# Results of two head groups packed into 32 rows, and VectorE's score blocks in threes, in a two-branch attention kernel

## The chip, the cores and the metric

The kernel runs on one core of a Trainium2 chip, as one program on its five engines: TensorE (PE in the profile), VectorE (DVE), ScalarE (ACT), GpSimd (POOL) and SyncE (SP), which issues the DMA transfers. The metric is the device time of one execution in microseconds (us). The kernel before took 934.92 us, the median of three runs (931.52, 934.92 and 940.07).

## What is computed

```python
def reference(A_x, A_wqkv, A_wo, B_x, B_wqkv, B_wo, gate_w):
    # B = 1, S = 2048, D = 512, H = 32 heads of Dh = 16
    def _A_ref(x, wqkv, wo):          # full attention
        q, k, v = split_heads(x @ wqkv)
        p = softmax(einsum("bhqd,bhkd->bhqk", q, k) * Dh ** -0.5)
        return merge_heads(einsum("bhqk,bhkd->bhqd", p, v)) @ wo
    def _B_ref(x, wqkv, wo):          # each query sees 8 keys, 2 apart, ending at itself
        q, k, v = split_heads(x @ wqkv)
        idx = pos[:, None] - 2 * arange(8)[None, :]
        logits = where(idx >= 0, einsum("bhsd,bhswd->bhsw", q, k[idx]) * Dh ** -0.5, -1e9)
        return merge_heads(einsum("bhsw,bhswd->bhsd", softmax(logits), v[idx])) @ wo
    g = sigmoid((A_x * gate_w).sum(-1, keepdims=True))
    return g * _A_ref(A_x, A_wqkv, A_wo) + (1 - g) * _B_ref(A_x, B_wqkv, B_wo)
```

All inputs and the output are bf16. Both branches read A_x. The work is the full attention of branch A: 32 heads x 2048 x 2048 scores and as many exponentials.

## The kernel before

**Tiling.** The 2048 queries are four chunks of 512. The 32 heads are eight groups of four (i = 0 to 7); the four heads j of a group lie in the four 32-row strips of the 128 partitions, 16 rows of data in each strip. A *period* is one head group on one chunk. There are 32: chunks 0 and 1 alternate through the eight groups (periods 0 to 15), then chunks 2 and 3 (16 to 31). A *block* is the scores of one head, 128 keys by 512 queries; a period has 64 of them (16 key tiles x 4 heads).

**The way of a block on ScalarE.** Blocks go in sets of 3 and 2 in turn. `qk` (L909) puts the scores of a set into one of two PSUM rings (tiles ring, rA of three banks and rB of two), one matmul a block; `ex` (L915) takes the exponential of the whole set in one ScalarE instruction into a tile pT (three buffers for each ring); `pv` (L928, through `pv_mm`, L876) multiplies each block with V and a column of ones into the accumulator acc, of which there is one PSUM bank. This leaves the result and the softmax's denominator of the four heads in acc, 17 rows of each strip.

**The way of a block on VectorE.** Some blocks of each period (`n_dve`, L20, 116 in all) are not given to ScalarE. `d_group` (L946, called from L1008) handles them in groups of up to two: `dq` puts the scores of one block into one of the two PSUM banks called misc, `p1` turns them to a scaled number in dt (one VectorE instruction a block), and `p2`, `p3` and `p4` form the exponential from it for the whole group (dg<-dt, dg<-dt,dg and pd<-dg,dt, scalar_tensor_tensor instructions over 512 elements a partition for each block of the group); `pv` multiplies pd into acc (called dpv). Each `dq` waits for the `p1` of the block before it. dt, dg and pd have one buffer each.

**The end of a period.** VectorE turns acc in 32 x 32 blocks into accT (`po1`), takes the reciprocal of the denominators (`pr`), multiplies (`po2`, L1028) into half of each 32-wide row of ott2, whose other half is zero, and turns ott2 back (`po3`, L1033) into its head group's plane of the tile oat. A plane has 128 rows, of which only 16 of each 32 carry data; woarr holds the matching rows of A_wo, with zeros in the others, so that the output product (`a_mm`, L1052, and `a_steps`, L1069; PE's misc_ps<-woarr,oat) takes eight planes, four matmuls of 32 output rows for each, for every 128 queries.

**Output.** For chunks 0 to 2 each tile of 128 queries is done once its chunk's last period is over: product with woarr (pf), scaled by the gate into fa, product of branch B with bwo (pb), sum into osb, store. For chunk 3, branch B's part is put into fb early, planes 0 to 3 (pf) and 4 to 6 (pg) are added to it by `fa_ev` (L1115) as they come, and after the last period only plane 7 (pt) is left.

**Branch B** runs beside all that, in 16 tiles (`b_tile`, L649) planned 46.7 us apart: projections on PE, products and weighted sums on POOL (prod, ob, obb), small steps on VectorE.

**Projections.** `q_proj` (L534, called from L586) makes the queries of one period into a tile qt (three buffers), `k_proj` the keys kt_all of one head group and chunk; both use the misc banks and VectorE.

**The order.** Every piece is an `Op` with an engine, an expected duration, a due time, dependencies and tokens for the buffers it takes (a token of a resource can only be given when the users of an older one are done). `list_schedule` (L80) lays all of them out in time with these expected durations, adds products with zeros where PE would otherwise be idle (acc<-ones_t,z, `zeros`), and the program is issued in that order; on each engine it is strict, and semaphores wait where a buffer or a result is not there yet. A changed duration, buffer count or due time so changes the order on every engine.

Of the kernel before, what the change touches and what calls it, by code (L numbers as in the profile page):

```python
# [9 lines left out]
ALU = mybir.AluOpType  # L10
# [8 lines left out]
    chunks_at_once=2,  # L19
    n_dve=(3,) * 14 + (2,) * 4 + (4,) * 9 + (6,) * 5,  # L20
    dve_tiles=2,
# [6 lines left out]
DH = 16  # L28
NG = 8
# [153 lines left out]
def kernel(  # L183
# [21 lines left out]
    NBG = S // 32  # L205
    BPC = QW // 32
    SZ = cfg["set_sizes"]
    NTD = cfg["dve_tiles"]
# [99 lines left out]
    z_scr = tc.dram_tile([S], FP32, name="z_scr")  # L308
    woarr = const.tile([128, NG, D], BF16, name="woarr")
    ident = const.tile([128, 128], BF16, name="ident")  # L310
# [24 lines left out]
    def init_dve():  # L335
        V.memset(selq[:], 0.0)
        V.memset(rowc[:], 0.0)
        for j in range(4):
            V.memset(selq[32 * j:32 * j + DH, 32 * j + DH:32 * j + DH + 1], 1.0)
            V.memset(rowc[32 * j:32 * j + DH + 1, 1:2], 1.0)  # L340
            V.memset(rowc[32 * j:32 * j + DH + 1, 2:3], SHIFT)
            V.memset(rowc[32 * j:32 * j + DH, 0:1], 1.0)
            V.memset(rowc[32 * j:32 * j + DH, 1:3], 0.0)
        V.memset(ott2[:], 0.0)

# [3 lines left out]
    def init_pool2():  # L349
        make_identity(nc, identf[:])  # L350
        G.memset(vp_all[:, 0, :, :], 1.0)
        G.memset(vp_all[:, 1:NT, :, DH:DH + 1], 1.0)

    def init_pool3():
        G.memset(woarr[:], 0.0)

# [3 lines left out]
    o_init_p = op("pool", 2.8, init_pool2, -8.0, deps=[o_id])  # L360
    o_wz = op("pool", 3.6, init_pool3, -7.0, deps=[o_init_p])

# [3 lines left out]
    def load_x(sc):  # L366
        def s():
            if sc < 2:
                xl = work.tile([128, W, D], BF16, name="xld", tag="prod", bufs=2)
            else:  # L370
                xl = work.tile([128, NG, QW], BF16, name="xld2", tag="oat", bufs=2)
            SP.dma_start(out=xl[:, 0:TPC, :], in_=x2d[sc * QW:(sc + 1) * QW, :].rearrange("(t p) d -> p t d", p=128))
            xld[sc] = xl
        return s
# [11 lines left out]
    def load_wo():  # L386
        SP.dma_start(out=bwo[:], in_=B_wo.rearrange("(c p) n -> p c n", p=128))
        wo4 = A_wo.rearrange("(i j d) n -> j d i n", j=4, d=DH)
        for j in range(4):
            SP.dma_start(out=woarr[32 * j:32 * j + DH, :, :], in_=wo4[j])  # L390
        SP.dma_start(out=v_scr[0:16, :], in_=woarr[16:32, 0, :])

# [9 lines left out]
    o_bw = op("sp", 1.0, load_bw, -8.3, lat=14.5)  # L402
    o_wo = op("sp", 3.5, load_wo, -8.2, deps=[o_wz], lat=17.0)

# [129 lines left out]
    def q_proj(pi, tag, dl, rel=0.0):  # L534
        c_, i = periods[pi]
        st = {}
        tk = tok(tag, 2 if tag == "misc" else 1)
        tq = tok("qt", 3)
        ta = tok("absq", 1)
        q_tok[pi] = tq  # L540

        def part(c0, c1):
            def s():
                if c0 == 0:
                    st["p1"] = misc_ps([128, QW], tag=tag)
                    st["absq"] = work.tile([128, QW], BF16, name="absq", tag="absq", bufs=1)
                    qt_tiles[pi] = work.tile([128, QW], BF16, name="qt", tag="qt", bufs=3)
                for c in range(c0, c1):
                    mm_heads(st["p1"], c, 4 * i * DH, xT[:, c, c_ * QW:(c_ + 1) * QW], c == 0, c == DC - 1)
            return s  # L550
# [34 lines left out]
    for pi in range(1, NP):  # L585
        q_proj(pi, "misc", S0[pi] - 16.0, rel=S0[pi - 1] + 4.0 if pi == 1 else S0[pi - 1] - 4.0)  # L586

# [311 lines left out]
    for k, us in enumerate(sets):  # L899
# [4 lines left out]
        tr_ = tok(ring, 1)  # L904
        tp = tok("pT" + ring, 3)
        tn = T0 + UNIT * sum(SZ) * (k // 2) + (UNIT * SZ[0] if k % 2 else 0)
# [8 lines left out]
        def ex(us=us, st=st, ring=ring, maxn=maxn, n=n):  # L915
            st["p"] = work.tile([128, maxn, QW], BF16, name="pT", tag="pT" + ring, bufs=3)
            A.activation(out=st["p"][:, 0:n, :], in_=st["r"][:, 0:n, :], func=ACT.Exp, scale=float(DH) ** -0.5)
# [25 lines left out]

    d_last = [None]

    def d_group(pi, gr, lo, hi):  # L946
        c_, i = periods[pi]
        n = len(gr)
        st = {}
        td, tg, tp = tok("dt", 1), tok("dg", 1), tok("pd", 1)  # L950

# [9 lines left out]
        def p1(q_):  # L961
            def s():
                if q_ == 0:
                    st["dt"] = work.tile([128, 2, QW], FP32, name="dt", tag="dt", bufs=1)
                    st["fr"] = st["dt"][:].bitcast(U16).rearrange("p u (n two) -> p u n two", two=2)[:, 0:n, :, 0]
# [4 lines left out]
        def p2():  # L970
            st["dg"] = work.tile([128, 2, QW], BF16, name="dg", tag="dg", bufs=1)
            V.scalar_tensor_tensor(out=st["dg"][:, 0:n, :], in0=st["fr"], scalar=EXP_A, in1=st["fr"],
                                   op0=ALU.subtract, op1=ALU.mult)
# [5 lines left out]
        def p4():  # L979
            st["pd"] = work.tile([128, 2, QW], BF16, name="pd", tag="pd", bufs=1)  # L980
            V.scalar_tensor_tensor(out=st["pd"][:, 0:n, :].bitcast(U16), in0=st["dg"][:, 0:n, :], scalar=EXP_C,
# [6 lines left out]
        def dur(t):  # L988
            return 0.15 + 0.535 * n + ((0.2 + 0.16 * n) if in_b(t) else 0.05)
        prev = d_last[0]  # L990
        for q_, (t, j) in enumerate(gr):
            tx = tok("misc", 2)
            a = op("pe", 0.28, dq(q_), hi - 7.5 + q_, dense=0.75, deps=[o_q[pi], o_kc[i][t // TPC], prev] + ([o_k0[t // TPC]] if i == 0 else []), alloc=[tx], use=[q_tok[pi]],
                   rel=lo, lat=0.52, name=f"dq{pi}")
            prev = op("dve", 0.70, p1(q_), hi - 6.5 + q_, deps=[a], alloc=[td] if q_ == 0 else [],
                      use=[tx] + ([td] if q_ else []))
        d_last[0] = prev
        a = op("dve", dur, p2, hi - 4.2, deps=[prev], alloc=[tg], use=[td])
# [5 lines left out]
    for pi in range(NP):  # L1004
        gs = [dorder[u_:min(u_ + 2, n_dve[pi])] for u_ in range(0, n_dve[pi], 2)]
        plen = S0[pi + 1] - S0[pi]
        for m, gr in enumerate(gs):
            d_group(pi, gr, S0[pi] - 6.0, S0[pi] + 1.0 + (plen - 7.0) * (m + 1) / len(gs))  # L1008


    oat_tiles, oat_tok, o_oat = {}, {}, {}
    for pi, (c_, i) in enumerate(periods):
        st = {}
        if i == 0:
            oat_tok[c_] = tok("oat", 2)
        ta, to = tok("accT", 2), tok("ott", 2)
        E = S0[pi + 1]
# [9 lines left out]

        def po2(pi=pi, st=st):  # L1028
            rden = st["rden"]
            rd_bc = _ap(rden[:], [list(rden[:].ap[0]), [1, BPC], [0, DH]])  # L1030
            V.tensor_tensor(out=ott2[:, pi % 2, :, 0:DH], in0=st["a"][:, :, 0:DH], in1=rd_bc, op=ALU.mult)

        def po3(pi=pi, c_=c_, i=i):  # L1033
            if c_ not in oat_tiles:
                oat_tiles[c_] = work.tile([128, NG, QW], BF16, name="oat", tag="oat", bufs=2)
            V.transpose(out=oat_tiles[c_][:, i, :], in_=ott2[:, pi % 2].rearrange("p b d -> p (b d)"))
        prev = [o_oat[pi - 1]] if pi else []
        a = op("dve", 0.75, po1, E - 1.0, deps=o_pv[pi], alloc=[ta], use=[acc_tok[pi]])
        a = op("dve", 0.27, pr, E + 3.5, deps=[a], use=[ta])
        a = op("dve", 0.60, po2, E + 4.0, deps=[a], alloc=[to], use=[ta])  # L1040
        o_oat[pi] = op("dve", 0.74, po3, E + 6.0, deps=[a] + prev, alloc=[oat_tok[c_]] if i == 0 else [],
                       use=[to] + ([oat_tok[c_]] if i else []))

    st_fb = {}
    for t in range(NT):
# [41 lines left out]
        if not last:  # L1087
# [7 lines left out]
            def b_ev(st=st, t=t):  # L1095
# [3 lines left out]
                                       op0=ALU.mult, op1=ALU.add)  # L1099
            a, tk = a_steps("pf", 0, NG, dl - 2.0, [o_oat[PL], o_g, o_wo] + o_obt[TPC * c_:TPC * (c_ + 1)], [oat_tok[c_]])  # L1100
            tf = tok("accT", 2)
# [34 lines left out]
        o_fb = op("dve", 0.70, fb_ev, dl + 1.0, deps=[a, o_g], alloc=[] if tt else [tfb], use=[tk] + ([tfb] if tt else []))  # L1136
        dl = S0[NP - 3] + 5.0 * tt
        a, tk = a_steps("pf", 0, 4, dl, [o_oat[p_of[c_, 3]], o_fb, o_g], [oat_tok[c_]])
        a = op("dve", 0.75, fa_ev("pf"), dl + 1.0, deps=[a, o_fb], use=[tk, tfb])
        dl = S0[NP - 1] + 8.0 + 3.0 * tt  # L1140
        b, tk = a_steps("pg", 4, NG - 1, dl, [o_oat[p_of[c_, NG - 2]], a], [oat_tok[c_]])
        a = op("dve", 0.75, fa_ev("pg"), dl + 1.0, deps=[a, b], use=[tk])
        tag = ("misc", "acc", "misc", "rA")[tt]
        tk, tos = tok(tag, 2 if tag == "misc" else 1), tok(otag, obufs)
        E2 = S0[NP]
        b = op("pe", 0.26, a_mm("pt", NG - 1, NG, True, True, tag=tag), E2 + tt, deps=[o_oat[NP - 1], a], alloc=[tk], use=[oat_tok[c_]])
        b = op("dve", 0.70, t_ev, E2 + 1 + tt, deps=[b, a], alloc=[tos], use=[tk, tfb])
# [39 lines left out]
```

## Time and profile before

| | before |
|---|---|
| median of three runs | 934.92 us |
| profiled execution | 930.82 us |
| its span, first to last instruction | 929.0 us |
| ScalarE busy | 890.4 us (96%) |
| TensorE busy | 837.3 us (90%) |
| VectorE busy | 656.9 us (71%) |
| GpSimd busy | 524.9 us (57%) |
| mean granted TensorE clock | 0.99 |
| exponentials of score sets on ScalarE | 773, 880.5 us in all |

Lines of groups read: engine, operation, what is written <- what is read by the program's names, shapes (partitions x elements), number of instructions, then busy us and mean ns of one, then the engine's idle time just before them and what ended it. Nearly every instruction goes through one recording helper, so the line number (L240, L249) says little and the tile's name says which step it is. In lines of stretches each engine has its busy us and its instructions in brackets; after the engines stand the granted clock of TensorE as a share, the share of the DMA engines, and GB/s. In lines of waits the three figures are us in total, times and the longest.

### The profile page before, as it was taken

How to read it: one execution, taken by the hardware profiler on the slowest of the kernel's cores; microseconds unless marked ns; L12 is line 12 of the kernel's file. 1: busy time of each engine (PE TensorE's matmuls, PEld its weight loads, DVE VectorE, ACT ScalarE, POOL GpSimd, SP SyncE). 2: the span in 40 equal slices, each digit the busy share in tenths (PEclk: the TensorE clock that was granted, in tenths of full speed). 3: DMA queues.
4: the chain of work that ended last, by engine and by line, in shares of the span. 5: the costliest groups of instructions: out<-in, count | busy, mean ns of one | idle time of the engine just before them, and what ended most of it. 6: DMA issues, size and time to landing. Idle time of an engine off the chain costs nothing.

```text
span 929.0 us, 20631 instructions
## 1 busy us (share of the span) xinstructions
PE 837.3 (90%) x8716; PEld 312.5 (34%) x8716; DVE 656.9 (71%) x880; ACT 890.4 (96%) x799; POOL 524.9 (57%) x412
## 2 busy tenths in 40 slices
PE   7999999989998999989999988888989898889887
PEld 4333334333433334333333432332323322222222
DVE  4676787887588777776436575778687876577676
ACT  4999999999999999999998999999999999999994
POOL 3445682868558748685854393989694993000000
PEclk9999999999999999999999999999999989999999
DMA  9101010010101010100012001010110010000001
GB/s 272 53 2 52 2 53 2 7 46 7 52 3 47 22 37 2 52 24 30 6 65 69 13 2 52 1 52 2 52 47 7 1 46 1 1 1 2 1 1 47
DMA packets 27269, 28.62 MB, mean 31 GB/s; under 512 B 1540, under 2 KB 26660, under 8 KB 27176
## 3 DMA queue, kind: packets, MB, share of 16 engines
q1 hardware_dynamic: 27176, 27.30, 9.2%
q8 instruction: 68, 1.11, 0.5%
q14 instruction: 25, 0.20, 0.1%
HBM read 23.08 MB, written 4.22 MB: 29 GB/s over the span
## 4 chain that ended last, share of the span: by engine, by line
ACT 50%; issue 20%; PE 20%; DVE 9%; DMA 1%; SPq 0%; ACTq 0%; DVEq 0%
ACT pT L240 49%; PE misc_ps L249 6%; PE ring L249 6%; PE acc L249 5%; DVE dg L240 4%; DVE pd L240 1%; PE misc L249 1%; DVE dt L240 1%; DMA xld<-in_A_x_dram 1%; ACT lg L240 1%; DVE osb L240 0%; DVE qt L240 0%; DVE accT L240 0%; DVE vd_all L240 0%; DVE ott L240 0%
## 5 line engine op out<-in xcount | busy, mean ns | idle before, releaser
L240 ACT ACTIVATE pT<-ring 128x1536 bf16<-128x1536 f32 (+1 forms) x773 | 880.5, 1347 | 15.5 <-PE acc L249 8.4
L249 PE MATMUL ring<-qt,kt_all 32*128 32x512 bf16 x1932 | 307.9, 383 | 72.4 <-ACT pT L240 65.7
L249 PE MATMUL acc<-pT,vp_all 128*17 128x512 bf16 (+1 forms) x1932 | 306.1, 385 | 0.6 <-DVE accT L240 0.2
L249 PEld LDWEIGHTS <-kt_all 32*128 32x128 bf16 x2048 | 114.3, 91 | 343.8 <-issue 330.4
L240 POOL TENSOR_TENSOR prod<-kTb,qTb 128x512 f32<-128x512 bf16 x128 | 165.0, 1311 | 106.4 <-DVE qTb L240 84.6
L240 POOL TENSOR_TENSOR prod<-vsh,lg 128x512 f32<-128x512 bf16 x128 | 170.5, 1355 | 0.8
L240 DVE TENSOR_SCALAR dt<-misc 128x512 f32<-128x512 f32 x116 | 79.7, 687 | 71.5 <-PE misc L249 65.6
L240 POOL TENSOR_TENSOR prod<-prod 128x512 f32<-128x512 f32 x80 | 122.7, 1549 | 1.3
L249 PEld LDWEIGHTS <-vp_all 128*17 128x17 bf16 (+1 forms) x1932 | 67.8, 88 | 122.6 <-issue 113.2
L240 DVE SCALAR_TENSOR_TENSOR pd<-dg,dt 128x1024 uint16<-128x1024 bf16 x65 | 98.3, 1513 | 1.7 <-PE acc L249 0.6
L240 DVE SCALAR_TENSOR_TENSOR dg<-dt,dg 128x1024 bf16<-128x1024 uint16 x65 | 96.3, 1482 | 1.6
L249 PE MATMUL misc_ps<-xT,wst 128*32 128x512 bf16 x1024 | 94.0, 382 | 1.1 <-ACT kt_all L240 0.8
L240 DVE SCALAR_TENSOR_TENSOR dg<-dt 128x1024 bf16<-128x1024 uint16 x65 | 91.8, 1412 | 1.7
L240 POOL TENSOR_TENSOR lg<-lg,rr 128x256 f32<-128x256 f32 x16 | 10.4, 648 | 126.8 <-ACT pT L240 60.0
L249 PE MATMUL acc<-ones_t,z 128*32 128x512 bf16 x211 | 74.6, 393 | 0.0
L249 PE MATMUL misc<-qt,kt_all 32*128 32x512 bf16 x116 | 44.9, 387 | 0.9 <-DVE kt_all L240 0.6
L249 PE MATMUL misc_ps<-woarr,oat 128*32 128x512 bf16 x512 | 44.1, 382 | 1.6 <-DVE fa L240 1.6
L249 PE MATMUL misc_ps<-prod,hsel 128*32 128x128 f32 x1024 | 42.9, 279 | 0.7 <-DVE kt_all L240 0.3
L249 PE MATMUL misc_ps<-xT,bw 128*128 128x128 bf16 x512 | 38.5, 220 | 0.0
L249 PEld LDWEIGHTS <-bw 128*128 128x128 bf16 x512 | 28.8, 98 | 14.7 <-issue 14.1
L249 PEld LDWEIGHTS <-wst 128*32 128x32 bf16 x1024 | 25.5, 95 | 22.2 <-issue 10.7
L249 PE MATMUL acc<-pd,vd_all 128*17 128x512 bf16 x116 | 27.6, 382 | 5.1 <-DVE pd L240 3.2
(86 smaller groups left out, 608.3 us busy)
## 6 DMA issues: line engine op xcount, KB each, us to landing
vsh<-v_scr SPq DMA_DIRECT2D x16, 1024.0 KB, 5.1
xld<-in_A_x_dram SPq DMA_DIRECT2D x4, 512.0 KB, 4.0
v_scr<-vs SPq DMA_DIRECT2D x16, 128.0 KB, 1.7
out_dram<-osb SPq DMA_DIRECT2D x16, 128.0 KB, 1.7
wst<-in_A_wqkv_dram SPq DMA_DIRECT2D x3, 512.0 KB, 8.8
bw<-in_B_wqkv_dram SPq DMA_DIRECT2D x1, 1536.0 KB, 11.2
bwo<-in_B_wo_dram SPq DMA_DIRECT2D x1, 512.0 KB
woarr<-in_A_wo_dram SPq DMA_DIRECT2D x4, 128.0 KB, 11.8
```

The lines of the kernel that those rows point to most:

```text
L240: return chain_on(key, f(*a, **k))
L249: return chain(nc.tensor.matmul(out, lhsT=lhsT, rhs=rhs, start=start, stop=stop, **kw))
```

## The change

The 16 rows of an odd head group go into the free half of the rows of the even one before it. `po2` of group i writes half i % 2 of the rows of ott2 (which is still one tile for each of the two chunks at work), and `po3` turns it back once for two groups, after the odd one. So oat and woarr have four planes and no zero rows, the output product is four planes long, and chunk 3's has two parts in place of three: planes 0 to 2 ahead of time, plane 3 at the end. woarr is loaded in eight transfers of 64 KB in place of four of 128 KB, is not zeroed any more, and the zero rows for the head of v_scr come from a tile osb that POOL zeroes.

VectorE's blocks go in groups of up to three of near equal size (a period with 3 blocks has one group, with 5 a pair and a triple, with 6 two triples), and there are 129: 3 each in periods 0 to 17, 5 each in 18 to 26, 6 each in 27 to 31. `dq` waits for the `p1` of the block before the last one. pd gets three buffers, pT four for each ring, qt four. A group may start 25 us ahead of its period's planned start in place of 6, and the queries are due 4 us earlier and may start 8 us earlier. The expected duration of `p2` to `p4` while branch B runs changes from 0.35 + 0.695 us x blocks to 0.51 + 0.535 us x blocks.

```diff
-    n_dve=(3,) * 14 + (2,) * 4 + (4,) * 9 + (6,) * 5,
+    n_dve=(3,) * 18 + (5,) * 9 + (6,) * 5,
...
+    NP2 = NG // 2
...
-    woarr = const.tile([128, NG, D], BF16, name="woarr")
+    woarr = const.tile([128, NP2, D], BF16, name="woarr")
...
-        V.memset(ott2[:], 0.0)
...
-        G.memset(woarr[:], 0.0)
+        st_z["z"] = work.tile([128, D], BF16, name="osb", tag="osb", bufs=2)
+        G.memset(st_z["z"][0:16, :], 0.0)
...
-        wo4 = A_wo.rearrange("(i j d) n -> j d i n", j=4, d=DH)
-        for j in range(4):
-            SP.dma_start(out=woarr[32 * j:32 * j + DH, :, :], in_=wo4[j])
-        SP.dma_start(out=v_scr[0:16, :], in_=woarr[16:32, 0, :])
+        wo5 = A_wo.rearrange("(m s j d) n -> s j d m n", s=2, j=4, d=DH)
+        for s_ in range(2):
+            for j in range(4):
+                SP.dma_start(out=woarr[32 * j + DH * s_:32 * j + DH * (s_ + 1), :, :], in_=wo5[s_][j])
+        SP.dma_start(out=v_scr[0:16, :], in_=st_z["z"][0:16, :])
...
-        tq = tok("qt", 3)
+        tq = tok("qt", 4)
...
-        q_proj(pi, "misc", S0[pi] - 16.0, rel=S0[pi - 1] + 4.0 if pi == 1 else S0[pi - 1] - 4.0)
+        q_proj(pi, "misc", S0[pi] - 20.0, rel=S0[pi - 1] + 4.0 if pi == 1 else S0[pi - 1] - 12.0)
...
-        tp = tok("pT" + ring, 3)
+        tp = tok("pT" + ring, 4)
...
-        td, tg, tp = tok("dt", 1), tok("dg", 1), tok("pd", 1)
+        td, tg, tp = tok("dt", 1), tok("dg", 1), tok("pd", 3)
...
-            return 0.15 + 0.535 * n + ((0.2 + 0.16 * n) if in_b(t) else 0.05)
-        prev = d_last[0]
+            return 0.15 + 0.535 * n + (0.36 if in_b(t) else 0.05)
+        prev2, prev = d_last
         for q_, (t, j) in enumerate(gr):
             tx = tok("misc", 2)
-            a = op("pe", 0.28, dq(q_), hi - 7.5 + q_, dense=0.75, deps=[o_q[pi], o_kc[i][t // TPC], prev] + ([o_k0[t // TPC]] if i == 0 else []), alloc=[tx], use=[q_tok[pi]],
+            a = op("pe", 0.28, dq(q_), hi - 7.5 + q_, dense=0.75, deps=[o_q[pi], o_kc[i][t // TPC], prev2] + ([o_k0[t // TPC]] if i == 0 else []), alloc=[tx], use=[q_tok[pi]],
...
-        gs = [dorder[u_:min(u_ + 2, n_dve[pi])] for u_ in range(0, n_dve[pi], 2)]
+        ng = -(-n_dve[pi] // 3)
+        gs = [dorder[m * n_dve[pi] // ng:(m + 1) * n_dve[pi] // ng] for m in range(ng)]
...
-            d_group(pi, gr, S0[pi] - 6.0, S0[pi] + 1.0 + (plen - 7.0) * (m + 1) / len(gs))
+            d_group(pi, gr, S0[pi] - 25.0, S0[pi] + 1.0 + (plen - 7.0) * (m + 1) / len(gs))
...
-            V.tensor_tensor(out=ott2[:, pi % 2, :, 0:DH], in0=st["a"][:, :, 0:DH], in1=rd_bc, op=ALU.mult)
+            V.tensor_tensor(out=ott2[:, pi % 2, :, DH * (i % 2):DH * (i % 2 + 1)], in0=st["a"][:, :, 0:DH], in1=rd_bc, op=ALU.mult)
...
-            V.transpose(out=oat_tiles[c_][:, i, :], in_=ott2[:, pi % 2].rearrange("p b d -> p (b d)"))
+            V.transpose(out=oat_tiles[c_][:, i // 2, :], in_=ott2[:, pi % 2].rearrange("p b d -> p (b d)"))
...
-        o_oat[pi] = op("dve", 0.74, po3, E + 6.0, deps=[a] + prev, alloc=[oat_tok[c_]] if i == 0 else [],
-                       use=[to] + ([oat_tok[c_]] if i else []))
+        if i % 2:
+            o_oat[pi] = op("dve", 0.74, po3, E + 6.0, deps=[o_po2[pi], o_po2[p_of[c_, i - 1]]], alloc=[oat_tok[c_]] if i == 1 else [],
+                           use=[to] + ([oat_tok[c_]] if i > 1 else []))
...
-            a, tk = a_steps("pf", 0, NG, dl - 2.0, [o_oat[PL], o_g, o_wo] + o_obt[TPC * c_:TPC * (c_ + 1)], [oat_tok[c_]])
+            a, tk = a_steps("pf", 0, NP2, dl - 2.0, [o_oat[PL], o_g, o_wo] + o_obt[TPC * c_:TPC * (c_ + 1)], [oat_tok[c_]])
...
-        dl = S0[NP - 3] + 5.0 * tt
-        a, tk = a_steps("pf", 0, 4, dl, [o_oat[p_of[c_, 3]], o_fb, o_g], [oat_tok[c_]])
+        dl = S0[NP - 3] + 9.0 * tt
+        a, tk = a_steps("pf", 0, NP2 - 1, dl, [o_oat[p_of[c_, NG - 3]], o_fb, o_g], [oat_tok[c_]])
         a = op("dve", 0.75, fa_ev("pf"), dl + 1.0, deps=[a, o_fb], use=[tk, tfb])
-        dl = S0[NP - 1] + 8.0 + 3.0 * tt
-        b, tk = a_steps("pg", 4, NG - 1, dl, [o_oat[p_of[c_, NG - 2]], a], [oat_tok[c_]])
-        a = op("dve", 0.75, fa_ev("pg"), dl + 1.0, deps=[a, b], use=[tk])
...
-        b = op("pe", 0.26, a_mm("pt", NG - 1, NG, True, True, tag=tag), E2 + tt, deps=[o_oat[NP - 1], a], alloc=[tk], use=[oat_tok[c_]])
+        b = op("pe", 0.26, a_mm("pt", NP2 - 1, NP2, True, True, tag=tag), E2 + tt, deps=[o_oat[NP - 1], a], alloc=[tk], use=[oat_tok[c_]])
```

## The prediction

> **What bounds the kernel now.** First the page, for the busy shares; then the waits of ScalarE (ACT) and its timeline, for what it loses; then the stretches, for where the other engines are full; last the groups with their forms apart, for prices.
>
> ```profile
> PE 837.3 (90%) x8716; PEld 312.5 (34%) x8716; DVE 656.9 (71%) x880; ACT 890.4 (96%) x799; POOL 524.9 (57%) x412
> ...
> L240 ACT ACTIVATE pT<-ring 128x1536 bf16<-128x1536 f32 (+1 forms) x773 | 880.5, 1347 | 15.5 <-PE acc L249 8.4
> ...
> L249 PE MATMUL misc_ps<-woarr,oat 128*32 128x512 bf16 x512 | 44.1, 382 | 1.6 <-DVE fa L240 1.6
> ```
>
> ACT is busy for 96% of the span, nearly all of it with the exponentials of 1932 blocks: 880.5 / 1932 = 0.4557 us a block. It runs from 20.28 to 916.46 us; what lies outside is 20.3 us of start and 12.5 us of tail. Its waits in between:
>
> ```profile
> ACT pT L240 <- PE acc L249: 8.4, 9, 2.0
> ACT pT L240 <- PE ring L249: 6.2, 12, 1.6
> ```
>
> "PE acc" means that all pT tiles were still full: TensorE (PE) was late with the products that empty them. "PE ring" means that the scores were late. In ACT's timeline the largest of the first kind stand together at the switch from chunks 0 and 1 to 2 and 3:
>
> ```profile
> 497.27 2.37 ACT L240 ACTIVATE pT<-ring 128x1536 bf16<-128x1536 f32 x2 [1.96 <-PE acc L249]
> ...
> 500.76 6.95 ACT L240 ACTIVATE pT<-ring 128x1536 bf16<-128x1536 f32 x6 [1.12 <-PE acc L249]
> ...
> 516.68 10.49 ACT L240 ACTIVATE pT<-ring 128x1536 bf16<-128x1536 f32 x9 [1.31 <-PE acc L249]
> ```
>
> All gaps between 484 and 517 add up to 6.2 us; those at 55, 82 and 271 us (0.83, 1.09, 0.59) to 2.5. In the timeline of PE from 480 to 517 output products (woarr and bwo) stand between scores and pT products.
>
> ```profile
> 400.00:500.00 100.00, 90.89 (x1067) 33.78 (x1064) 50.94 (x75) 96.57 (x87) 62.77 (x57) 1.00 0.13 42
> ...
> 600.00:700.00 100.00, 88.34 (x843) 31.90 (x841) 77.58 (x85) 98.41 (x90) 88.54 (x61) 0.98 0.11 35
> ...
> 916.50:929.00 12.50, 6.93 (x104) 2.63 (x99) 8.12 (x13) 0.00 (x0) 0.00 (x0) 0.82 0.19 64
> ```
>
> The columns are PE, weight loads, VectorE (DVE), ACT, POOL, then the granted clock. DVE is fullest (78%) in periods 18 to 26, about 536 to 786 us, which is where the change gives it more; POOL has nothing left after about 775 us.
>
> **The change, part by part.** The sum is against the profiled execution: 930.82 us, of which the span is 929.0. It lies 4.1 us under the median of the three runs (934.92), so the same difference is taken off that median.
>
> *129 blocks in place of 116.* Thirteen blocks leave ACT (1932 to 1919): 13 x 0.4557 = **-5.9 us**, on the path wherever ACT is full.
>
> *Half as many woarr products, and a fourth pT tile.* 512 matmuls become 256. Eight of them start in 0.43 us (483.06 to 483.50 in PE's timeline), so 256 are 13.8 us of PE, off the path except where they pile up. The built order shows piles: in before the heaviest four score sets in a row (ACT needs 4 x 1.139 = 4.56 us for four) carry 95 matmuls of 512 columns, 95 x 0.054 = 5.1 us, and with the short ones between them about 6.0 us; in the changed order the heaviest four carry 75, 4.1 us, and lie elsewhere. No run of four is then over ACT's time. So the 6.2 us at the switch should go, less 1.0 that I leave for order; of the other 2.5 us the fourth pT tile should cover 1.8: **-7.0 us**, between 0 (the waits return under another name) and -8.6.
>
> *Blocks in threes.* Prices by form:
>
> ```profile
> L240 DVE SCALAR_TENSOR_TENSOR dg<-dt,dg 128x1024 bf16<-128x1024 uint16 x51 | 82.1, 1610 | 1.3
> L240 DVE SCALAR_TENSOR_TENSOR pd<-dg,dt 128x1024 uint16<-128x1024 bf16 x51 | 82.0, 1607 | 1.2 <-PE acc L249 0.3
> ...
> L240 DVE SCALAR_TENSOR_TENSOR pd<-dg,dt 128x512 uint16<-128x512 bf16 x14 | 16.4, 1169 | 0.5 <-PE acc L249 0.3
> ...
> L240 DVE SCALAR_TENSOR_TENSOR dg<-dt,dg 128x512 bf16<-128x512 uint16 x14 | 14.2, 1014 | 0.3
> ```
>
> All three steps together: a pair 1.574 us, a single 1.086. From 800 to 900 us, without POOL, a pair takes 1.22, so some 0.35 us of the mean is time lost to POOL, and as singles lose about as much as pairs (0.69 without POOL) I take it as fixed for each instruction. A triple is then 1.574 + 0.53 = 2.10 us. Before: 65 groups, 286.4 us. After: 37 triples and 9 pairs, 3 x (37 x 2.10 + 9 x 1.574) = 275.6. With 13 more first steps (+8.9), 16 fewer transposes of ott (16 x 0.706 = -11.3), 4 fewer fb sums (-3.0) and no memset of ott (-0.5), DVE goes from 656.9 to about 640. That is off the path. If the loss to POOL grew with width, a triple would be 1.75 x 1.574 / 1.22 = 2.26 and DVE 18 us fuller, which only the third rival below would feel. The Trainium skill, SBUF - State Buffer, section "Who interferes with whom", says that an instruction of DVE with two SBUF inputs and a reading one of GpSimd exclude each other for whole instructions; by that rule the wait does not depend on the waiting one's width, and the rows of singles and pairs agree.
>
> What the stage shows: from 600 to 700 us DVE is busy for 77.6 us, which is 21.2 a period of 60 blocks (27.3 us). With five blocks for four a period has one more first step (0.69), one pair turned into a triple (3 x 0.53) and half a transpose less (0.35): 23.1 of 59 x 0.4557 = 26.9 us, or 86%. DVE's own order is strict, so what stands behind a triple waits up to 0.5 us longer than behind a pair: the turn of acc, for which PE's first product of the next period waits, and the reads that free the two misc banks, for which the next score block or projection on PE waits, and the ring scores behind it. PE's waits for DVE are small now (3.2 us for pd, 7 times; 0.6 and less for banks). Asking two ahead puts a score block into PE's queue one first step earlier, so a late DVE would now hold PE there. Three pd tiles, a fourth qt and the earlier start give DVE room. I take **+1.0 us**, between 0 and the third rival's 20.8.
>
> *Tail.* Before, after PE's last pd product (917.62):
>
> ```profile
> 917.65 0.72 DVE L240 STREAM_TRANSPOSE accT<-acc 128x512 f32<-128x512 f32 x1 [0.48 <-PE acc L249]
> ...
> 922.57 0.74 DVE L240 TENSOR_SCALAR fa<-misc_ps,g_sp 128x512 f32<-128x512 f32 x1
> ...
> 925.45 0.75 DVE L240 SCALAR_TENSOR_TENSOR osb<-misc_ps,omg,fa 128x512 bf16<-128x512 f32 x1 [0.82 <-PE misc_ps L249]
> ```
>
> Twelve DVE instructions with two waits on PE, then 2.8 us for the last store. In before two of chunk 2's output tiles come behind the end, in the changed order one: ten DVE instructions remain, 0.72 + 0.24 + 0.43 + 0.71 + 0.74 + 4 x 0.70 + 0.75 = 6.4 us, with 0.3 of gaps, 0.6 from the last exponential to the turn (1.19 before) and 2.8 of store: 10.0 for 12.5, **-2.5 us** (between -1 and -3.5, by whether the waits of 0.82 and 1.57 us on the way stay).
>
> *At nothing.* woarr comes in eight transfers, four more issues of SP at 0.69 us: SP is free at 14.9 us now and would be at 17.7; its next work is at 26.66. POOL's memset of woarr (3.81 us) goes; POOL's first product waits for qTb, not for it. First exponential at 20.28 as before. POOL may wait longer behind a triple (1.75 for 1.22 us), but the DVE instructions that can block it get fewer (195 to 138); its slack is its long waits for qTb (84.6 us in 15).
>
> Sum: -5.9 - 7.0 + 1.0 - 2.5 = **-14.4 us**: 916.4 for the profiled execution, 934.9 - 14.4 = 920.5 against the median.
>
> **Rivals.**
> *The waits return (chance 0.19).* PE is busy 90% and stays so; the fourth tile only lets ACT run one set further ahead, and a PE that is behind then shows as "PE ring". Then only 5.9 + 2.5 = 8.4 us come: 926.5. Against it: the heaviest pile falls under ACT's time.
>
> *The clock drops more often (0.13).*
>
> ```profile
> L249 PE MATMUL ring<-qt,kt_all 32*128 32x512 bf16 x10 | 2.6, 601 | 0.2 <-ACT pT L240 0.2
> ```
>
> That is a score matmul from 751 to 757 us; from 800 to 900 it takes 380 ns. Three such stretches (559.5, 634.3 and 750.8 us, 13.6 us long in all) hold 3.0 us of ACT's waits, and one more of 0.5 follows: 0.26 us for each us. With 256 matmuls fewer PE could fall there more often; 40 us of it would cost 7 more: 927.5. Against it: the built order adds five idle products, and the halved work lies where PE is fullest. The Trainium skill, TensorE: Matmul & The Clock Gate, Part 1, says that PE falls to half its clock after a window of about 3.4 us with too little activity; the lengths of 3.4 to 6.5 us agree.
>
> *DVE becomes the bound in periods 18 to 26, and the kernel slower (0.15).* The place: the dpv products at each period's end and the turn of acc behind them. Now 6.1 us of a 27.3 us period is DVE's idle time, mostly waits for PE that its strict order cannot fill; after the change 3.8 us are left. If all 6.1 are needed, each period grows by 2.3 us, nine by 20.8 in place of the 1.0 above: 940.3. It decides from 1.7 us a period on (15.4 / 9). Against it: the blocks may start 25 us ahead in place of 6, and DVE's work in periods 0 to 13 falls.
>
> **How the numbers follow.** Forecast 0.53 at **920.5 us**, returning waits 0.19 at 926.5, clock 0.13 at 927.5, DVE 0.15 at 940.3. The forecast's own bounds are 934.9 - 5.9 - 8.6 - 3.5 = 916.9 and, with a new wait of 5 in place of 1, 924.5; below them the clock's 3.5 us could go too, 913.4. The range **912 to 932** leaves out DVE's case and 0.05 at the ends of the others. A measurement tells about 1% (9.3 us) from no change: faster means under 925.6. Forecast 0.50 of its 0.53, a third of the two middle cases, 0.10: **0.60 faster**; the rest of those and 0.04 of DVE's, **0.29 same**; the rest of DVE's, as no row ends that queue at 940, **0.11 slower**.
>
> **What would show it.** 1919 blocks at 0.456 us on ACT; its "PE acc" waits under 2 us and none over 1 us between 480 and 520; the tail after the last exponential near 10 us; triples at 2.1 us with POOL and 1.75 without; 256 woarr matmuls; first exponential near 20.3. Wrong: ACT idle for over 10 us before pT; waits of PE for pd, accT or the misc banks of several us between 536 and 786; clock under 0.97 in several stretches; triples over 2.3.

## The result, and the profile after

The changed kernel takes 940.97 us, the median of 14 executions, beside 934.83 us for the kernel before: a ratio of 1.0058, 95% interval 1.003 to 1.0087. It is 0.6% slower (0.3 to 0.9%), where 920.5 us, 1.5% faster, was forecast. The profiled execution has a span of 939.4 us, 10.4 more than before.

The page after, and ScalarE's waits:

```profile
PE 838.8 (89%) x8465; PEld 308.6 (33%) x8465; DVE 659.3 (70%) x815; ACT 887.4 (94%) x794; POOL 550.6 (59%) x412
...
L241 ACT ACTIVATE pT<-ring 128x1536 bf16<-128x1536 f32 (+2 forms) x768 | 877.3, 1338 | 30.8 <-PE ring L250 25.8
```
```profile
ACT pT L241 <- PE ring L250: 25.8, 39, 1.7
...
ACT pT L241 <- PE acc L250: 4.1, 3, 2.3
```

The waits for full pT tiles ("PE acc") were halved, from 8.4 to 4.1 us. But ScalarE (ACT) now waits 25.8 us in 39 places for scores ("PE ring"), where it waited 6.2 us in 12. The whole balance in the span: exponentials 877.3 - 880.5 = -3.2; ScalarE's idle time before them 30.8 - 15.5 = +15.3; first exponential at 21.72 in place of 20.28, +1.4; tail 939.4 - 930.2 = 9.2 in place of 12.5, -3.3. Together +10.2 of the measured +10.4.

One place shows how such a wait comes about. The timeline of the changed kernel from 98 to 108 us (start, us, engine, what; in brackets the idle time before and its releaser):

```profile
98.18 2.71 DVE L241 SCALAR_TENSOR_TENSOR dg<-dt,dg 128x1536 bf16<-128x1536 uint16 x1
...
100.92 2.71 DVE L241 SCALAR_TENSOR_TENSOR pd<-dg,dt 128x1536 uint16<-128x1536 bf16 x1
...
101.48 0.39 PE L250 MATMUL ring<-qt,kt_all 32*128 32x512 bf16 x2 [0.20 <-ACT pT L241]
...
103.68 0.60 PE L250 MATMUL acc<-pd,vd_all 128*17 128x512 bf16 x3 [1.28 <-DVE pd L241]
...
104.22 1.03 PE L250 MATMUL ring<-qt,kt_all 32*128 32x512 bf16 x3
...
105.35 1.45 ACT L241 ACTIVATE pT<-ring 128x1536 bf16<-128x1536 f32 x1 [1.66 <-PE ring L250]
...
107.64 0.60 PE L250 MATMUL misc<-qt,kt_all 32*128 32x512 bf16 x1
```

Two VectorE instructions over three blocks take 2.71 us each while GpSimd works; the order had reckoned with 2.12. pd is late, TensorE stands for 1.28 us before the products with it, and the next three scores, which are behind them in its strict queue, come late and slowly: a single matmul of 512 columns takes 0.60 us from there on, where it took 0.39. The stretches show the clock of such places:

```profile
100.14:103.55 3.41, 1.98 (x18) 0.73 (x15) 3.38 (x2) 3.41 (x4) 3.41 (x2) 1.00 0.00 0
103.55:110.38 6.83, 6.70 (x53) 2.38 (x52) 3.92 (x7) 4.06 (x4) 2.19 (x3) 0.50 0.01 2
```
```profile
100.00:112.00 12.00, 10.43 (x97) 4.07 (x95) 8.24 (x11) 8.64 (x8) 5.74 (x4) 0.72 0.01 1
648.00:666.00 18.00, 15.95 (x112) 4.34 (x111) 11.53 (x13) 14.72 (x13) 14.44 (x10) 0.72 0.01 1
```

From 103.55 to 110.38 us the granted clock is 0.50, behind 3.41 us in which TensorE was busy for only 1.98; the 0.72 of the longer stretches is a mean over both clocks. The trace's record of the clock has ten such slow stretches at 0.50 between the first exponential and the tail, of 3.4, 6.8 or 10.2 us and 61.4 us in all, where before had three of 13.7 us. Of ScalarE's waits, 19.9 us lie in them or begin within 1.5 us behind; before it was 3.0. And TensorE's waits for VectorE:

```profile
PE acc L250 <- DVE pd L241: 13.5, 17, 2.0
...
PE acc L250 <- DVE accT L241: 2.4, 6, 0.7
```

Before, pd cost it 3.2 us in 7 waits, none longer than 0.7:

```profile
PE acc L249 <- DVE pd L240: 3.2, 7, 0.7
```

### The profile page after: what moved, and what is told of

It is laid out like the page before. It is cut to its first block, busy times and chain, and to the rows that moved or that the text cites. A ratio compares the mean times of both kernels' runs of the same rounds, so it can differ in the third digit from the quotient of the medians.

```text
span 939.4 us, 20046 instructions
## 1 busy us (share of the span) xinstructions
PE 838.8 (89%) x8465; PEld 308.6 (33%) x8465; DVE 659.3 (70%) x815; ACT 887.4 (94%) x794; POOL 550.6 (59%) x412
## 4 chain that ended last, share of the span: by engine, by line
ACT 42%; PE 21%; DVE 18%; issue 16%; DMA 1%; SPq 0%; DVEq 0%; ACTq 0%
ACT pT L241 41%; DVE dg L241 9%; PE ring L250 7%; PE acc L250 7%; PE misc_ps L250 6%; DVE pd L241 4%; DVE dt L241 2%; PE misc L250 1%; ACT lg L241 1%; DMA xld<-in_A_x_dram 1%; DVE qt L241 1%; DVE absq L241 1%; DVE accT L241 1%; DVE osb L241 0%; PE misc_ps L858 0%
## 5 line engine op out<-in xcount | busy, mean ns | idle before, releaser
L241 ACT ACTIVATE pT<-ring 128x1536 bf16<-128x1536 f32 (+2 forms) x768 | 877.3, 1338 | 30.8 <-PE ring L250 25.8
L250 PE MATMUL ring<-qt,kt_all 32*128 32x512 bf16 x1919 | 312.9, 391 | 65.8 <-ACT pT L241 59.2
L250 PE MATMUL acc<-pT,vp_all 128*17 128x512 bf16 (+1 forms) x1919 | 311.9, 395 | 2.5 <-DVE accT L241 2.4
L241 DVE TENSOR_SCALAR dt<-misc 128x512 f32<-128x512 f32 x129 | 86.3, 685 | 42.7 <-PE misc L250 34.7
L241 DVE SCALAR_TENSOR_TENSOR dg<-dt,dg 128x1536 bf16<-128x1536 uint16 (+1 forms) x46 | 98.3, 2137 | 0.9
L241 DVE SCALAR_TENSOR_TENSOR pd<-dg,dt 128x1536 uint16<-128x1536 bf16 (+1 forms) x46 | 97.5, 2120 | 1.0
L241 DVE SCALAR_TENSOR_TENSOR dg<-dt 128x1536 bf16<-128x1536 uint16 (+1 forms) x46 | 89.2, 1938 | 1.4
L241 POOL TENSOR_TENSOR lg<-lg,rr 128x256 f32<-128x256 f32 x16 | 13.5, 841 | 120.5 <-DVE rr L241 76.4
L241 DVE TENSOR_SCALAR qt<-misc_ps,rowc 128x512 bf16<-128x512 f32 x32 | 25.7, 804 | 29.5 <-PE misc_ps L250 29.4
L241 DVE TENSOR_SCALAR kt_all<-misc_ps,rowc 128x512 bf16<-128x512 f32 x28 | 22.6, 806 | 30.2 <-PE misc_ps L250 30.0
L250 PEld LDWEIGHTS misc_ps<-prod,hsel 128*32 128x32 f32 x1024 | 30.5, 118 | 14.6 <-issue 10.6
```

The costliest lines, as they stand in the source:

```text
L241: return chain_on(key, f(*a, **k))
L250: return chain(nc.tensor.matmul(out, lhsT=lhsT, rhs=rhs, start=start, stop=stop, **kw))
```

## The experiments

Ratios are to the kernel before, run on the same chip, with 95% intervals. The first theory was A: the order is laid out on VectorE times that are too short, TensorE stops for pd, and the stops lower its clock. Its rival B: half the output products are gone, and TensorE has too little to do to keep its clock.

**The packing alone** (e1_pack_only). All of the change but VectorE's part, which goes back:

```diff
-    n_dve=(3,) * 18 + (5,) * 9 + (6,) * 5,
+    n_dve=(3,) * 14 + (2,) * 4 + (4,) * 9 + (6,) * 5,
...
-            return 0.15 + 0.535 * n + (0.36 if in_b(t) else 0.05)
+            return 0.15 + 0.535 * n + ((0.2 + 0.16 * n) if in_b(t) else 0.05)
...
+        gs = [dorder[u_:min(u_ + 2, n_dve[pi])] for u_ in range(0, n_dve[pi], 2)]
...
+            d_group(pi, gr, S0[pi] - 6.0, S0[pi] + 1.0 + (plen - 7.0) * (m + 1) / len(gs))
```

(and one block ahead, three pT and qt, one pd, queries as before).

> The packing alone: results of two head groups in 32 rows, four planes of woarr, the tail in two parts; VectorE's blocks, their number (116), groups of two, one ahead, and all buffers as in the kernel before. Theory A (TensorE stops at the product that waits for pd, because a group of three takes VectorE longer than the order was laid out for; the stop makes the clock drop, and the slow stretch costs ScalarE): nothing of that is in this kernel, so 925 to 932 us, 2 to 9 below the kernel before, clock 0.98 or more, TensorE's waits for pd under 5 us in all. Theory B (with 256 products fewer TensorE has too little to do and its clock drops): 938 us or more, clock under 0.975, slow stretches of over 30 us.

Measured: 925.3 us, ratio 0.9919 (0.9892 to 0.9947). ScalarE's waits in it:

```profile
ACT pT L241 <- PE ring L250: 13.9, 19, 2.6
...
ACT pT L241 <- PE acc L250: 0.8, 1, 0.8
```

The waits for full pT tiles are nearly gone with three buffers, so the fourth was not needed for that; the waits for scores are 13.9 us where they were 6.2. The time is as A has it, and B's 938 us is wrong. The clock of the profiled execution is as B has it: 0.971, with 41 us of slow stretches behind the first exponential. Over the 12 executions the clock was 0.971 to 0.993 with a median of 0.979, beside 0.986 for the kernel before that ran with it; whether fewer products or another order lowered it is not shown, since the kernel before in another order (c4_before_nudge, below) has 0.981.

**The product with pd planned later** (e2_late_dpv).

```diff
-        a = op("dve", dur, p4, hi - 1.0, deps=[a], alloc=[tp], use=[tg, td])
+        a = op("dve", dur, p4, hi - 1.0, deps=[a], alloc=[tp], use=[tg, td], lat=0.15 + 0.535 * n + 2.2)
```

(and p1 waits for the p1 before it in its group.)

> The changed kernel, but the order takes the last step of a group (pd) to be there later: its latency is set to 0.15 + 0.535 x blocks + 2.2 us (3.96 for three, where the order had 1.81 to 2.12), so that the product with pd stands later in TensorE's queue; VectorE's own planned times are as in the changed kernel. Theory A: TensorE's waits for pd fall from 13.5 us to 2 to 5, the slow stretches from 55 us to under 30, ScalarE's waits for ring scores from 25.8 us to under 15, and the time from 941 to 922 to 932 us. Theory B: the waits for pd go, but the clock stays under 0.975 and the time at 937 to 943 us.

Measured: 940.9 us, ratio 1.0086 (1.0055 to 1.0117). TensorE's waits for pd are gone from its list of waits, and nothing is won: ScalarE waits 18.6 us for scores and 7.8 for pT tiles, and the slow stretches stay at 54.6 us. The time is B's (937 to 943 us) and not A's (922 to 932). The stop in front of pd is therefore not the cause by itself.

**Expected durations that fit** (e3_dur).

```diff
-            return 0.15 + 0.535 * n + (0.36 if in_b(t) else 0.05)
+            return 0.15 + 0.535 * n + (0.70 if in_b(t) else 0.05)
```

> The changed kernel with the expected duration of the steps of a group while branch B runs raised by 0.34 us (0.85 + 0.535 x blocks: 2.46 us for three, where the profile has a mean of 2.41 with GpSimd at work and the order had 2.12). This moves both VectorE's planned times and TensorE's products with pd. Theory A: 920 to 930 us, waits for pd under 6 us, clock 0.98 or more. Theory B: 937 to 943 us, clock under 0.975.

Measured: 930.9 us, ratio 0.9974 (0.9952 to 0.9995), waits for pd 1.8 us, clock 0.978. That is just outside of A's time and clock and far from B's time; taken alone this spoke for A.

**More idle products** (e6_fill).

```diff
-SPAN, ACTIVE, FILL, FILL1 = 3.4, 8.6, 0.25, 0.10
+SPAN, ACTIVE, FILL, FILL1 = 3.4, 10.2, 0.25, 0.10
```

> The changed kernel with more idle products: the order's threshold of activity is 10.2 where it was 8.6, which makes 458 products with zeros of 216. Theory A: a product with zeros stands in the same strict queue and cannot fill a stop of it; the waits for pd stay at 10 us or more, and the time at 936 us or more. Theory B: the clock goes back to 0.985 or more, and the time to 922 to 932 us.

Measured: 959.2 us, ratio 1.0285 (1.0253 to 1.0318). The profiled execution, with 950.1 us the fastest of eight, has a clock of 0.993 and only 10 us of slow stretches; the other seven have 0.979 to 0.988. Yet ScalarE waits 23.8 us for full pT tiles, and the waits for pd are 15.6 us. That the 242 further zeros put TensorE behind is likely but not shown: in those waits of ScalarE themselves zeros are 3.1 us of TensorE's work. The time is against B; a higher clock bought in this way cost more than it brought.

**One piece of VectorE's part at a time**, each put on the packing alone: 129 blocks (e7_pack_129, only `n_dve`), the change's durations (e8_pack_short, only `dur`), groups of three (e9_pack_threes, the lines for `gs` and a fitting `dur`), buffers and early starts (e11_pack_bufs).

```diff
-        gs = [dorder[u_:min(u_ + 2, n_dve[pi])] for u_ in range(0, n_dve[pi], 2)]
+        ng = -(-n_dve[pi] // 3)
+        gs = [dorder[m * n_dve[pi] // ng:(m + 1) * n_dve[pi] // ng] for m in range(ng)]
```

> The packing alone with 129 blocks in place of 116, in pairs, one ahead, with the old durations. Theory A (the loss comes from an order laid out on too short VectorE times): the durations are the old ones, so the thirteen blocks bring what they take from ScalarE, 13 x 0.456 = 5.9 us: 918 to 922 us where the packing alone took 925.3, waits of TensorE for pd under 4 us. Rival C (VectorE has no room for 129 blocks in any form): 928 us or more, ScalarE's idle time before pT over 22 us.

> The packing alone with one more line of the change: the expected duration of a group's steps while branch B runs, 0.51 + 0.535 x blocks in place of 0.35 + 0.695 x blocks, so 1.58 us for a pair where it was 1.74 and the profile's mean with GpSimd at work is 1.86. Theory A: 930 to 935 us where the packing alone took 925.3, TensorE's waits for pd 4 us or more in place of 0.6. If it stays at 923 to 928 us, the duration matters only in groups of three.

> The packing alone with groups of up to three (18 triples and 31 pairs: 3 blocks as one group, 4 as two pairs, 6 as two triples), still 116 blocks, one ahead, and with the expected duration that fits the profile, 0.85 + 0.535 x blocks. Theory A: groups of three are no loss when the order knows their time, 922 to 928 us. Rival D (long VectorE instructions hold up what stands behind them, whatever the order expects): 931 us or more.

> The packing alone with the buffers and early starts of the change: four pT a ring, four qt, three pd, groups from 25 us and queries from 12 us ahead; pairs, 116, one ahead, old durations. Theory A: these are no loss, 921 to 927 us. Rival E (the early starts bring VectorE's and the misc banks' work forward of what is urgent): 930 us or more, with longer waits of VectorE's qt and kt_all for TensorE than in the packing alone (19.1 and 16.4 us).

Measured, in this order: 932.8, 935.9, 935.3 and 931.4 us; ratios 0.9988 (0.9963 to 1.0013), 1.001 (0.9984 to 1.0036), 1.0028 (1.0008 to 1.0048) and 0.9984 (0.9964 to 1.0005). The rivals C, D and E have their times; in the second, A's waits for pd came (6.0 us), and the time is just over A's range. Each is slower than the packing alone (0.9919), and they can't all be causes that add up: together they would give more than the change. So the orders themselves had to be tried.

**The same kernels in another order.** Branch B's planned start is moved; no work and no duration changes.

```diff
-    b_start=26.0,
+    b_start=26.6,
```

> A control: the packing alone with the planned start of branch B moved from 26.0 to 26.6 us, which changes no work and no duration but lets the order come out differently. Theory A (planned VectorE times too short make TensorE stop, the stop lowers the clock): 922 to 929 us, as the packing alone (925.3). Rival F (each order has its own time by chance, and the packing alone had a good one): 930 us or more.

> A control: the changed kernel with the same move of branch B by 0.6 us. Theory A: 937 to 943 us with a clock of 0.96 to 0.97 and 10 us or more of waits for pd, as the changed kernel (941.0). Rival F: it can fall anywhere between 928 and 945; below 935 the loss of the change would be one of its order, not of the change.

> A control: the changed kernel with the expected duration that fits the profile (0.85 + 0.535 x blocks), and the same move of branch B by 0.6 us. Theory A: 927 to 934 us and at least 6 us under the changed kernel with the same move. Rival F: no such order between the two.

> A control: the kernel before with the same move of branch B by 0.6 us. Under every theory that holds the orders to be alike, 930 to 936 us (before: 932.5 to 934.8). Rival F: outside of that, which gives the size of the scatter between orders.

Measured: the packing alone 924.3 us, the changed kernel 926.4, the one with fitting durations 936.4, the kernel before 935.0. The packing alone and the kernel before are where theories without a scatter have them. But the changed kernel became 1.3% faster, below even rival F's 928 us, and the one with fitting durations became slower, as F allows and A does not. Theory A has fallen in this form: in that order the kernel with fitting durations waits 0.5 us for pd and still has slow stretches of 61.4 us. Two more orders, 25.4 (d1a_after, d2a_pack) and 27.2 us (d1b_after, d2b_pack):

> The changed kernel with branch B's planned start at 25.4 us in place of 26.0. Theory F (what the change does to the work is a gain of some 6 to 10 us, and each order adds 0 to 16 us by waits and clock): 925 to 938 us, and with the other three orders a mean under 933.7, the kernel before. Theory G (the change loses, and 926.4 was the exception): 936 us or more.

> The changed kernel with branch B's planned start at 27.2 us. Theory F: 925 to 938 us. Theory G: 936 us or more. In either case the time goes with the clock, 4 to 5 us for each 0.01 from about 926 us at 0.983.

> The packing alone with branch B's planned start at 25.4 us. The packing's own gain (tail 3 to 4 us, waits at the switch of chunks 5 to 6) is in every order: 920 to 930 us. If it is over 932, the 925.3 and 924.3 of its first two orders were chance too.

> The packing alone with branch B's planned start at 27.2 us: 920 to 930 us by the packing's own gain; over 932 if that was chance.

Measured: the changed kernel 940.7 and 946.6 us, both in G's range and out of F's; the packing 930.1 and 929.1 us, at the upper end of what was expected. The last sentence on the clock fails too: at 0.956, the median of d1b_after, it gives 937 to 940 us.

And the two largest pieces in a second order, 26.6:

> The packing alone with 129 blocks in pairs, and branch B's planned start at 26.6 us. If the thirteen blocks are a gain in themselves (5.9 us) and the 0.9988 of their first order was chance: 917 to 922 us, under the packing alone in this order (924.3). If ScalarE's waits take the gain back whatever the order: 926 to 935 us, ScalarE idle for 5 us or more beyond the 9.0 of the packing alone.

> The packing alone with groups of up to three, 116 blocks, durations that fit the profile, and branch B's planned start at 26.6 us. If groups of three lose in themselves: 930 us or more, with ScalarE waiting over 8 us for full pT tiles (12.3 us in the first order, 0.2 in the packing alone). If the 935.3 of the first order was chance: 922 to 928 us.

Measured: 937.3 us with thirteen blocks more, over both of the ranges (ScalarE is idle for 26.8 us before its exponentials, 11.7 in the packing alone in this order), and 942.0 us with groups of three, which lose in themselves by what was expected.

All ratios side by side:

| | 26.0 | 26.6 | 25.4 | 27.2 |
|---|---|---|---|---|
| kernel before | 1 | 1.0018 | | |
| packing alone | 0.9919 | 0.9904 | 0.9972 | 0.9950 |
| changed kernel | 1.0058 | 0.9932 | 1.0068 | 1.0130 |
| its TensorE waits for pd, us | 13.5 | 7.6 | 15.0 | 16.0 |
| the same, packing alone | 0.6 | 0.8 | 4.7 | 1.9 |
| changed, fitting durations | 0.9974 | 1.0024 | | |
| packing and 129 blocks | 0.9988 | 1.0017 | | |
| packing and groups of three | 1.0028 | 1.0095 | | |

Intervals of the new ones: packing 0.9868 to 0.9939, 0.9946 to 0.9999, 0.9923 to 0.9977; changed 0.9904 to 0.996, 1.004 to 1.0095, 1.0091 to 1.0169; before 0.9991 to 1.0044; fitting 0.9994 to 1.0055; 129 0.9983 to 1.0052; threes 1.0066 to 1.0124.

The packing has a mean of 0.9936 over four orders (standard deviation 0.0031) and is under 1 in each; the changed kernel has 1.0047 (0.0083). In each order the changed kernel is slower than the packing alone, by 0.0028 to 0.018, 0.0111 in the mean; the smallest, in order 26.6, is within the noise. So the loss is VectorE's part of the change, with its buffers and early starts, in its size spread widely by the order; the packing is a gain. Whether the change as a whole loses against the kernel before is not shown over orders: 1.0047 is less than its scatter away from 1. Thirteen blocks more lose 0.7 and 1.1% against the packing in the same order, groups of three, with fitting durations, 1.1 and 1.9%.

How groups of three lose before any drop of the clock is seen in f2_threes_nudge, whose profiled execution has a mean clock of 0.987. Its timeline from 406.5 to 415 us:

```profile
409.01 2.54 DVE L241 SCALAR_TENSOR_TENSOR pd<-dg,dt 128x1536 uint16<-128x1536 bf16 x1
...
411.60 0.39 PE L250 MATMUL acc<-pd,vd_all 128*17 128x512 bf16 x3 [1.80 <-DVE pd L241]
...
412.91 0.71 DVE L241 STREAM_TRANSPOSE accT<-acc 128x512 f32<-128x512 f32 x1
...
413.67 1.03 PE L250 MATMUL acc<-pT,vp_all 128*32 128x512 bf16 x7 [0.30 <-DVE accT L241]
...
414.36 1.02 ACT L241 ACTIVATE pT<-ring 128x1024 bf16<-128x1024 f32 x1 [6.19 <-PE acc L250]
```

This is the end of a period. Its last group is now three blocks wide, three instructions of 2.5 us one after the other; only then can its products go into acc, only then is acc turned, and only then can the next period's products empty the pT tiles, which are all full (three for each ring). ScalarE stands for 6.19 us. The clock's record drops to 0.50 at 413.67 us only, behind 3.41 us with TensorE busy for 1.44. Of the 17.7 us that ScalarE waits for full pT tiles, in six places, four waits at the ends of periods make 16.2. It is 12.0 us in the kernel's first order; in the packing alone it was 0.8 and 0.2 us:

```profile
ACT pT L241 <- PE acc L250: 17.7, 6, 6.2
```

## Why the prediction was wrong

The step that failed is the new wait: "I take **+1.0 us**, between 0 and the third rival's 20.8". ScalarE's waits for late scores rose by 19.6 us (25.8 - 6.2), almost the upper end. Term by term, measured for forecast: thirteen blocks -3.2 for -5.9; waits for full pT tiles -4.3 for -7.0; the new wait +19.6 for +1.0; tail -3.3 for -2.5; first exponential +1.4, which stood at nothing and whose cause stays open. That is +10.2 for -14.4 us.

The prediction saw that a late VectorE would hold TensorE's strict queue, and that TensorE's waits for VectorE were small; but it took the second for a sign that the first would stay harmless. TensorE's waits for pd went from 3.2 to 13.5 us, and 19.9 us of ScalarE's waits are in or just behind stretches at half the clock, where 3.0 were. VectorE's load, reckoned at 640 us, is off the path, though it is 659.3: the three steps of all groups took 285.0 us where 275.6 were reckoned. The places shown above point to the time from a group's first step to its products, not to the load; that the waits for pd alone made the loss is not so, by e2_late_dpv.

- *The triple's price.* Forecast "a triple is then 1.574 + 0.53 = 2.10 us"; the means of the three steps are 2.044, 2.247 and 2.207:

```profile
L241 DVE SCALAR_TENSOR_TENSOR dg<-dt,dg 128x1536 bf16<-128x1536 uint16 x37 | 83.1, 2247 | 0.8
L241 DVE SCALAR_TENSOR_TENSOR pd<-dg,dt 128x1536 uint16<-128x1536 bf16 x37 | 81.7, 2207 | 0.9
L241 DVE SCALAR_TENSOR_TENSOR dg<-dt 128x1536 bf16<-128x1536 uint16 x37 | 75.6, 2044 | 1.1
```

  Yet the mean hides what matters. With GpSimd at work for 90% of the instruction or more a triple takes 2.41 us and a pair before took 1.86, in the mean; with GpSimd idle, 1.754 and 1.217. "What would show it" had 2.1 for a triple with GpSimd; that took the mean of all pairs for that of the disturbed ones. The part that was argued from singles and pairs held: the loss to GpSimd is 0.66 us for a triple and 0.64 for a pair, and so hardly depends on the width. That agrees with the exclusive lock that the Trainium skill, SBUF — State Buffer, section "Who interferes with whom", states for the ports that the two engines share.
- *129 blocks, -5.9 us.* Busy time fell by 3.2 us, as a block took 877.3 / 1919 = 0.4572 us in place of 0.4557. As a gain in time there was none: put on the packing alone, the thirteen blocks cost 0.7 and 1.1% in two orders. TensorE's waits for pd are 7.5 and 8.2 us there, and ScalarE's for full pT tiles 7.1 and 8.1; each is under 1 us in the packing alone.
- *The packing, -7.0 and -2.5 us.* The mechanism was right for the waits that it names: in the four orders of the packing alone "PE acc" is 0.2 to 1.0 us, where it was 8.4, and the tail is 8.8 to 9.7 us, where it was 12.5. Its time is 0.64% (6 us) lower in the mean of the orders, 7.6 us in the first. But the 8.4 us were in part a matter of one order (3.0 in c4_before_nudge), and "PE ring", 6.2 before, is 9.9 to 18.5 us in these profiled executions (16.2 in c4_before_nudge), so that the full -7.0 is not shown. In the changed kernel the tail fell by 3.3 us where 2.5 was forecast (the items of that sum add up to 10.1, not 10.0), but three waits at the switch stayed, between 499 and 516 us, 4.1 us in all: "none over 1 us between 480 and 520" was wrong.
- *The clock rival* (0.13, "40 us of it would cost 7 more"). The slow stretches grew by 48 us (61.4 - 13.7), and ScalarE's waits in and just behind them by 17 (19.9 - 3.0): 0.35 us for each us, where 0.26 was reckoned, so its price was too small. Its cause, fewer products, explains a part at most: the packing alone, with as few, has 27 to 44 us of slow stretches in its four orders (the kernel before 13.7 and 30.7 in two) and still gains.
- *The third rival* (0.15) named the right place, the products at a period's end and the turn of acc behind them, and the periods in part: of the 25.8 us that ScalarE waits for scores in the changed kernel, 15.8 lie between 536 and 786 us (4.1 before), but 6 between 100 and 210. VectorE did not become the bound there: it was busy for 191.5 of these 250 us, 188.4 before, where 86% was reckoned. That its 940.3 us is so near to the 941.0 measured is luck. "Against it: the blocks may start 25 us ahead" did not help; e11_pack_bufs, with these early starts and pairs, lost as well.
- *The first rival*, that waits return under another name, happened as well: "PE acc" fell by 4.3 us while "PE ring" rose.
- *What the prediction did not reckon with at all* is that the same change can come out at 0.993 or at 1.013 by the order that the planner happens to find. A forecast of 1.5% for a re-planned kernel had a scatter of 0.3% (the packing alone) to 0.8% (the changed kernel) in it before any cost was counted.

What stays open: how the loss divides between thirteen blocks, groups of three, durations and early starts. Each loses alone, the last two in one order only, and the parts do not add up. Nor is the slow clock a matter of pd alone. In the 3.41 us ahead of its ten slow stretches TensorE of the changed kernel was idle for 15.1 us in all, 8.0 of them in waits for pd and 5.2 in waits for ScalarE. In c3_dur_nudge it was idle for 12.7 us ahead of eleven, 11.8 of them in waits for ScalarE and none for pd. A late pd is one way to leave TensorE idle at such a place; why one order has more such places than another is not known.

## What to carry to other kernels

Where a planner or a scheduler lays out the order, time a change in several orders (move something that has no cost) before giving its parts a price; here a move of 0.6 us in a plan moved the changed kernel by 1.3%. Making the pieces of an off-path engine larger saves its time but lengthens the chain at whose end something else is waiting; look for the last piece before a buffer turns over. And take an operation's price from the rows of the disturbed state in which it will run, not from the mean over disturbed and undisturbed ones.

## What the runs showed of the hardware

The executions of one program differ by the clock that TensorE is granted, and their times follow it closely. Over the 138 executions of the kernel before that stood beside the experiments, from 929.0 to 941.1 us, mean clocks ran from 0.972 to 0.996, with a correlation of -0.985 and 4.7 us for each 0.01: 930.9 us in the mean at 0.99 and more, 938.2 under 0.98. An idle TensorE can lengthen the time by itself as well as lower the clock, so the slope is not the price of the clock alone. The changed kernel's 14 executions had 0.954 to 0.970. An estimate from that slope: at a clock of 0.987, as the kernel before mostly had it, it would take 941.0 - 2.25 x 4.7 = 930 us, and 933 by the slope of its own 14 executions (3.6 us for each 0.01), still far from the forecast. By the same line the packing alone lies 5.8 to 11.0 us under the kernel before at a like clock in its four orders, and the changed kernel 0.0 to 9.2. The clock is not all, as f2_threes_nudge shows with 942.0 us at 0.986.

The clock fell without any long stop. In the changed kernel no single wait of TensorE for VectorE was over 2.0 us behind the start; in the 3.41 us ahead of its ten slow stretches TensorE was busy for 35 to 68%. In the clock records of all 20 traces every slow stretch that ends within the trace lasts one to eight times 3.413 us, and in each trace all of them start on one grid of that step. Taken window by window on this grid, from about 31 to 915 us, the clock was halved after 45 of 46 windows at full clock with TensorE busy under 60%, after 51 of 120 with 60 to 70%, and after 18 of 4772 with more. These shares are rough, as the ends of matmuls are modelled. The Trainium skill, TensorE: Matmul & The Clock Gate, section "HAM oscillation — how this bites in real kernels", puts the rule as no idle gap over about 3.4 us; in the changed kernel gaps of 2.0 us and less were enough.
